# Backward pass of a gated attention and ReGLU mix: three edits to how attention's probabilities are turned, how queries are spread, and where projections stand

## The chip, the cores and the metric

The kernel runs on one core of a Trainium2 chip. A core has five instruction streams that run side by side and meet at semaphores: TensorE (PE; its weight loads, PEld, overlap its matmuls), VectorE (DVE), ScalarE (ACT), GpSimd (POOL) and SyncE (SP), which here only issues DMAs. Matmuls write to PSUM; the other data lies in SBUF, 128 partitions wide. A DMA that is issued from SP or ACT costs that queue its issue time; one that is issued from GpSimd is an instruction in GpSimd's own order. The metric is the device time of one execution in microseconds (us). Before: median 954.69 us of 3 runs (953.86 to 954.94).

## The reference

The input x has 2048 rows of 512. Two branches work on it and a gate mixes them; the kernel computes the output and the gradients of x, of all weights and of the gate, for a given grad_out.

```python
g = _sigmoid((x * gate_w).sum(-1, keepdims=True))
# branch A: attention, 32 heads of 16, a row sees itself and the 255 rows before it
qkv = (x @ wqkv).reshape(B, S, 3, H, Dh)
scores = jnp.einsum("bhqd,bhkd->bhqk", q, k) * (Dh ** -0.5)
mask = (idx[:, None] - idx[None, :] >= 0) & (idx[:, None] - idx[None, :] < W)
p = _softmax(jnp.where(mask[None, None], scores, -1e9), axis=-1)
a = jnp.einsum("bhqk,bhkd->bhqd", p, v).transpose(0, 2, 1, 3).reshape(B, S, D) @ wo
# branch B: relu(x W_gate) * (x W_up), times W_down; F = 1376
b = jnp.einsum("bsf,fd->bsd", relu(gate) * up, W_down)
return g * a + (1 - g) * b

# and the result with its gradients
_out, _vjp = jax.vjp(_f, A_x, A_wqkv, A_wo, B_W_gate, B_W_up, B_W_down, gate_w)
return (_out, *_vjp(grad_out))
```

## The kernel before

The work has three stages. The first (to about 254 us) does branch B forward and its backward products, in 11 chunks of the hidden width by 4 groups of 512 rows. The third (from about 760 us) does the products that give the output and the gradient of x, 128 rows at a time. Neither has an edit in it, apart from how the first group of queries is written at its end.

The second stage is attention, forward and backward, and it holds the change. It loops over 4 chunks `c` of 8 heads, and in a chunk over 16 blocks `j` of 128 query rows. A block meets key blocks `kb` = j, j-1 and j-2, which are its roles: "d" (diagonal, masked from above), "m" (middle, no mask) and "f" (far, masked from below). The 8 heads of a chunk are taken as two halves of 4. A block has so 6 units, one for each role and half; their order is m, f, d for the first half and m, d, f for the second. There are 360 units in all, since the first two blocks of a chunk have fewer.

The order of all engines is written by hand, as a loop over slots `n` (`manual_schedule`: each engine keeps the order of the program). In slot n:

- `front(u)` of unit n: PE multiplies K of one half by the spread queries into ST (L616, 128 keys x 4 heads x 128 queries). ACT takes exp into Pu (L627). GpSimd masks Pu for the roles d and f (L629, L632).
- `gradp` of unit n-1: VectorE multiplies Pu by dPT into Pd (L646).
- `rowsum` of unit n-3: PE multiplies both by K and V into BA (L655, L657), the rows' sums, outputs and parts of the gradients. After a block's last unit ACT copies BA out, and VectorE and GpSimd make small scaled tiles from it over the next slots (`small_ops`, L705 to L723).
- `front_dp(u)`: PE makes dPT for unit n (L641).
- `cd_piece`: PE multiplies the turned Pu and Pd of an older unit by those scaled tiles into CD (L486, L489), the gradients of K and V.

CD needs Pu and Pd turned: queries on the partitions instead of keys. `flip` does this in one of two ways. On PE: 8 transposes into PSUM (L687) and a copy to SBUF, by ACT and VectorE in turn, in slot n+3 of the unit. By DMA: a transposing DMA that SP issues in slot n+2. Diagonal units go by DMA, both halves in one transfer (tile PPd, L671). Of the middle units only the first half goes by DMA, alone (tile PPm, L678), in chunks 0 to 2 and in the blocks before 10 of chunk 3 (`u.dma`, L604). All other units are turned on PE. PPd has 3 buffers, PPm 2.

Between these, a running `credit` of PE time puts in background work: the weight gradients of the chunk before (L572), and the projections for the next group of 512 rows (`project_parts`): Q (L128), dO (L131), a transposing DMA of both, K, V, and a set of transposes of K and V. One part may go into a slot. Q and dO land side by side in a tile `zT`. ST and dPT want the heads in separate columns, each head-pair's 32 partitions alone in one column block with zeros around it, and so `spread` copies 32 rows at a time from `zT` to the tile `z` (L468), by four DMAs for each group, two in the slot after dO's and two in the next. SP issues them. `z` has two buffers, one for each group in turn; 15 groups are spread so, and the first is copied by VectorE and ACT.

`M`, a pool of four PSUM buffers, serves ST, dPT, the projections and the weight gradients.

Of the kernel before, what the change touches and what calls it, by code (L numbers as in the profile page):

```python
# [11 lines left out]
BF = mybir.dt.bfloat16  # L12
# [10 lines left out]
def kernel(  # L23
# [80 lines left out]
    NP = P // 32  # L104
    ZB = 2
    wq = ctx.enter_context(tc.tile_pool(name="wq", bufs=1))
    zt = [wq.tile([P, 2, TPG, NP, P], BF, tag=f"z{i}", name=f"z{i}") for i in range(ZB)]
    pjA = ctx.enter_context(tc.tile_pool(name="pjA", bufs=1))
    pjs = {}
    pools = {}  # L110
# [1 line left out]
    if True:  # L112
# [5 lines left out]
        def project_parts(c, tg):  # L118
# [4 lines left out]
            def mm(nm, which, eng):  # L123
# [20 lines left out]
                if nm in ("Q", "dO"):  # L144
                    if c == 0 and tg == 0:
                        w = ("Q", "dO").index(nm)
                        for k in range(NP):
                            rows = slice(32 * k, 32 * k + 32)
                            evac(zt[0][rows, w, :, k, :], dst[rows, :].rearrange("p (k q) -> p k q", k=TPG),
                                 (("dve", "act")[w] if k % 2 else "dve"))  # L150
                else:
                    for k in range(2):
                        t4[f"{nm}{k}"] = pj.tile([P, TGW], BF, tag=f"{nm}{k}", name=f"{nm}{k}")
                        if PENG[k] == "act":
                            nc.scalar.mul(t4[f"{nm}{k}"][:], pp[:], par[:, k:k + 1])
                        elif PENG[k] == "dve":
                            nc.vector.tensor_scalar(t4[f"{nm}{k}"][:], pp[:], par[:, k:k + 1], None, op0=ALU.mult)
                        else:
                            nc.vector.tensor_scalar(t4[f"{nm}{k}"][:], dst[:], par[:, k:k + 1], None, op0=ALU.mult)
# [297 lines left out]
    if True:  # L457
# [7 lines left out]
        pools["now"] = (ps, "M", 4, "TR")  # L465
        def spread(gi, k):
            rows = slice(32 * k, 32 * k + 32)
            nc.sync.dma_start(zt[gi % ZB][rows, :, :, k, :],  # L468
                              proj[groups[gi]]["z"][rows, :, :].rearrange("p w (k q) -> p w k q", k=TPG))

        P2 = {}
        RQ = {}
# [120 lines left out]
        for c in range(DC):  # L593
            for j in range(NT):
                kbs = [k for k in (j - 1, j, j - 2) if k >= 0]
                for half in range(2):
                    order = kbs if half or len(kbs) < 3 else [kbs[0], kbs[2], kbs[1]]
                    for ki, kb in enumerate(order):
# [2 lines left out]
                        u.first = ki == 0 and half == 0  # L601
                        u.last = ki == len(kbs) - 1 and half == 1
                        u.role = ("d", "m", "f")[j - kb]
                        u.dma = u.role == "d" or (u.role == "m" and half == 0 and (c < DC - 1 or j < 10))  # L604
                        units.append(u)
        NU = len(units)

# [2 lines left out]
        def front(u):  # L610
# [2 lines left out]
            KTt = proj[(u.c, u.kb // TPG)][f"K{u.half}"]  # L613
            ksl = slice((u.kb % TPG) * P, (u.kb % TPG + 1) * P)
            ST = ps.tile([P, HH, P], F32, tag="M", bufs=4, name="ST")
            nc.tensor.matmul(ST[:], lhsT=KTt[:, ksl], rhs=z[:, 0, jl, :, :], start=True, stop=True)  # L616
            if u.role == "d":
                if u.half == 0:
                    pairs[(u.c, u.j)] = wk.tile([P, 2, 2, HH, P], BF, tag="PPd", bufs=3, name="PPd")
                u.PP = pairs[(u.c, u.j)][:, u.half, :, :, :]  # L620
                u.Pu, u.Pd = u.PP[:, 0, :, :], u.PP[:, 1, :, :]
            elif u.dma:
                u.PP = wk.tile([P, 2, HH, P], BF, tag="PPm", bufs=2, name="PPm")
                u.Pu, u.Pd = u.PP[:, 0, :, :], u.PP[:, 1, :, :]
            else:
                u.Pu = wk.tile([P, HH, P], BF, tag="Pu", bufs=3, name="Pu")
# [8 lines left out]
        def front_dp(u):  # L635
# [2 lines left out]
            VTt = proj[(u.c, u.kb // TPG)][f"V{u.half}"]  # L638
            ksl = slice((u.kb % TPG) * P, (u.kb % TPG + 1) * P)
            u.dPT = ps.tile([P, HH, P], F32, tag="M", bufs=4, name="dPT")  # L640
            nc.tensor.matmul(u.dPT[:], lhsT=VTt[:, ksl], rhs=z[:, 1, jl, :, :], start=True, stop=True)  # L641

        def gradp(u):
            if not u.dma:
# [19 lines left out]
        copier = {"i": 0}  # L664

        def flip(u):
            if u.role == "d":
                if u.half == 0:
                    return
                p2 = wk.tile([P, 2, 2, HH, P], BF, tag="P2d", bufs=4, name="p2d")  # L670
                nc.sync.dma_start_transpose(out=p2[:].rearrange("p b a h q -> p (b a h) q"),  # L671
                                            in_=pairs.pop((u.c, u.j))[:].rearrange("p b a h q -> p (b a h q)"))
                for b in range(2):
                    P2[(u.c, u.j, u.kb, b)] = p2[:, b, :, :, :]
                return
            if u.dma:
                p2 = wk.tile([P, 2, HH, P], BF, tag="P2m", bufs=6, name="p2")
                nc.sync.dma_start_transpose(out=p2[:].rearrange("p a h q -> p (a h) q"),  # L678
                                            in_=u.PP[:].rearrange("p a h q -> p (a h q)"))
                P2[(u.c, u.j, u.kb, u.half)] = p2  # L680
                return
            eng = ("act", "dve")[copier["i"] % 2]
            copier["i"] += 1
# [1 line left out]
            for a, src in enumerate((u.Pu, u.Pd)):  # L685
                for hh in range(HH):
                    nc.tensor.transpose(pt[:, a, hh, :], src[:, hh, :], ident[:])  # L687
            p2 = wk.tile([P, 2, HH, P], BF, tag=f"P2{u.role}", bufs={"m": 6, "f": 4}[u.role], name="p2")
            evac(p2[:], pt[:], eng)
            P2[(u.c, u.j, u.kb, u.half)] = p2  # L690

        def small_ops(c, j, s):
# [88 lines left out]
        with tc.manual_schedule():  # L781
# [7 lines left out]
            n = 0  # L789

            held = False
            early = []
            late = []

# [14 lines left out]
            while n <= NU + LAG or ev or cdq or bgq:  # L809
# [63 lines left out]
                elif held and credit > 0.3:  # L873
                    held = background()
                    credit -= 0.65
                elif prq and not held and (credit > 0.4 or due - n <= len(prq)):
                    credit -= (0.44, 0.86, 0.86, 0.1, 0.86, 0.86)[len(prq) - 1]
                    prq.pop(0)()
                    if len(prq) == 4:
# [154 lines left out]
```

## Time and profile before

One execution with the profiler on took 954.53 us; its span, first to last instruction, is 952.6 us.

| | whole span | 300 to 400 us | 400 to 500 us | 600 to 700 us |
|---|---|---|---|---|
| PE busy | 917.2 us, 96% | 95.6% | 98.6% | 97.1% |
| PEld busy | 586.9 us, 62% | 69.6% | 71.7% | 69.9% |
| DVE busy | 503.1 us, 53% | 70.7% | 71.4% | 68.5% |
| ACT busy | 458.6 us, 48% | 71.7% | 73.2% | 70.0% |
| POOL busy | 486.9 us, 51% | 71.0% | 66.5% | 66.3% |
| share of the 16 DMA engines | | 0.83 | 0.86 | 1.01 |

How to read it: the page gives busy time of each engine, the span in 40 slices, the chain of work that ended last, and groups of instructions by line with their mean time and the idle time just before them. Matmuls are pipelined, so a matmul's own duration (378 ns for 512 columns) is longer than the step to the next one; the timeline's start times tell what it costs. A DMA share near 1 counts time in which packets were under way, not bytes at full rate.

### The profile page before, as it was taken

How to read it: one execution, taken by the hardware profiler on the slowest of the kernel's cores; microseconds unless marked ns; L12 is line 12 of the kernel's file. 1: busy time of each engine (PE TensorE's matmuls, PEld its weight loads, DVE VectorE, ACT ScalarE, POOL GpSimd, SP SyncE). 2: the span in 40 equal slices, each digit the busy share in tenths (PEclk: the TensorE clock that was granted, in tenths of full speed). 3: DMA queues.
4: the chain of work that ended last, by engine and by line, in shares of the span. 5: the costliest groups of instructions: out<-in, count | busy, mean ns of one | idle time of the engine just before them, and what ended most of it. 6: DMA issues, size and time to landing. Idle time of an engine off the chain costs nothing.

```text
span 952.6 us, 26867 instructions
## 1 busy us (share of the span) xinstructions
PE 917.2 (96%) x10965; PEld 586.9 (62%) x11065; DVE 503.1 (53%) x921; ACT 458.6 (48%) x795; POOL 486.9 (51%) x935
## 2 busy tenths in 40 slices
PE   7999999999989999999999999989999999999998
PEld 4556566556557776677776777766777644444443
DVE  4433334334367777567776667766677322322223
ACT  5422322222368777667776667866688310000001
POOL 2645445444177666666777567775677411121111
PEclk9999999999999999999999999999999999999999
DMA  9998789998587796977997869899989599777741
GB/s 295 189 189 194 181 205 211 211 205 191 135 146 125 130 170 110 158 149 122 169 139 128 145 124 182 145 149 166 180 148 204 136 271 229 189 189 189 187 100 44
DMA packets 470835, 160.27 MB, mean 168 GB/s; under 512 B 399448, under 2 KB 468408, under 8 KB 470712
## 3 DMA queue, kind: packets, MB, share of 16 engines
q1 hardware_dynamic: 448312, 135.48, 75.4%
q10 hardware_dynamic: 20592, 17.84, 6.9%
q0 software_dynamic: 1808, 5.24, 1.6%
q8 instruction: 86, 1.41, 0.6%
q14 instruction: 37, 0.30, 0.1%
HBM read 32.15 MB, written 36.31 MB: 72 GB/s over the span
## 4 chain that ended last, share of the span: by engine, by line
PE 65%; POOL 11%; DMA 7%; DVE 6%; issue 5%; ACT 3%; SPq 2%; ACTq 0%; POOLq 0%; DVEq 0%
PE dxps L976 7%; PE pt L687 5%; PE ST L616 5%; PE wps L371 5%; PE dPT L641 5%; PE dxps L991 4%; PE wps L572 4%; PE pp L128 4%; PE bps L945 4%; POOL Pu L632 3%; PE dhps L324 3%; PE BA L655 3%; PE CD L486 2%; PE gps L324 2%; PE ups L324 2%
## 5 line engine op out<-in xcount | busy, mean ns | idle before, releaser
L646 DVE TENSOR_TENSOR Pd<-Pu,dPT 128x512 bf16<-128x512 bf16 x178 | 120.2, 678 | 62.2 <-POOL Pu L632 49.7
L616 PE MATMUL ST<-z,K 128*128 128x512 bf16 x354 | 133.7, 378 | 6.1 <-DVE Pd L646 2.0
L641 PE MATMUL dPT<-z,V 128*128 128x512 bf16 x348 | 131.5, 378 | 4.4 <-DVE Pd L646 2.3
L627 ACT ACTIVATE Pu<-ST 128x512 bf16<-128x512 f32 x178 | 107.6, 604 | 45.4 <-PE ST L616 35.3
L629 POOL TENSOR_SCALAR_AFFINE_SELECT PPd<-PPd 128x512 bf16<-128x512 bf16 x128 | 81.7, 639 | 70.6 <-ACT PPd L627 70.2
L338 POOL TENSOR_TENSOR hT<-rg,upm 128x512 bf16<-128x512 bf16 x44 | 51.6, 1173 | 119.0 <-DVE upm L336 92.1
L646 DVE TENSOR_TENSOR PPd<-PPd,dPT 128x512 bf16<-128x512 bf16 x128 | 87.4, 683 | 44.6 <-POOL PPd L629 43.0
L371 PE MATMUL wps<-dgu_r,x_r 128*128 128x256 bf16 x704 | 105.6, 273 | 1.8 <-DVE wst L74 1.0
L72 ACT COPY p<-pt 128x1024 bf16<-128x1024 bf16 x89 | 90.7, 1019 | 7.5 <-PE pt L687 4.9
L627 ACT ACTIVATE PPd<-ST 128x512 bf16<-128x512 f32 x128 | 77.1, 602 | 32.4 <-PE ST L616 31.4
L371 PEld LDWEIGHTS <-x_r 128*128 128x128 bf16 x704 | 68.8, 98 | 32.6 <-issue 2.1
L632 POOL TENSOR_SCALAR_AFFINE_SELECT Pu<-Pu 128x512 bf16<-128x512 bf16 x112 | 71.6, 639 | 23.6 <-ACT Pu L627 23.4
L954 ACT COPY a_sb<-aps 128x512 f32<-128x512 f32 x16 | 9.4, 586 | 153.2 <-issue 137.6
L336 DVE SCALAR_TENSOR_TENSOR upm<-rg,ups 128x512 bf16<-128x512 bf16 x44 | 30.1, 684 | 79.9 <-ACT rg L330 40.3
L687 PE MATMUL pt<-ident,Pd 128*128 128x128 bf16 x712 | 68.8, 219 | 0.0
L486 PE MATMUL CD<-rq,p 128*128 128x32 bf16 x928 | 68.1, 177 | 0.5
L330 ACT ACTIVATE rg<-gps 128x512 bf16<-128x512 f32 x44 | 26.3, 598 | 87.2 <-PE gps L324 48.8
L687 PE MATMUL pt<-ident,Pu 128*128 128x128 bf16 x712 | 68.2, 217 | 0.0
L489 PEld LDWEIGHTS <-p 128*128 128x128 bf16 x928 | 54.6, 96 | 19.5
L489 PE MATMUL CD<-rq,p 128*128 128x16 bf16 x928 | 66.6, 169 | 0.0
L74 DVE COPY p<-pt 128x1024 bf16<-128x1024 bf16 x89 | 60.8, 684 | 6.0 <-PE pt L687 5.9
L486 PEld LDWEIGHTS <-p 128*128 128x128 bf16 x928 | 61.9, 96 | 1.2 <-issue 1.1
(167 smaller groups left out, 2236.1 us busy)
## 6 DMA issues: line engine op xcount, KB each, us to landing
dqkvo_d<-rows_st SPq DMA_DIRECT2D x7, 1024.0 KB, 6.0
hT_d<-hT ACTq DMA_DIRECT2D x44, 128.0 KB, 2.5
dgT_d<-dgu ACTq DMA_DIRECT2D x44, 128.0 KB, 2.8
duT_d<-dgu ACTq DMA_DIRECT2D x44, 128.0 KB, 3.0
duT_g<-duT_d SPq DMA_DIRECT2D x8, 640.0 KB, 5.4
gt<-hT_d SPq DMA_DIRECT2D x7, 640.0 KB, 5.9
dgT_g<-dgT_d SPq DMA_DIRECT2D x7, 640.0 KB, 5.2
z<-zT SPq DMA_DIRECT2D x60, 64.0 KB, 2.2
```

What stands on the lines that cost most here:

```text
L72: nc.scalar.copy(out, in_)
L371: nc.tensor.matmul(acc["w"][:, c, :], lhsT=x_r[:, t, c * P:(c + 1) * P], rhs=k.dgu_r[:, :, i, :], start=(go_ and c % 2 == 0), stop=no_, sk ...
L486: nc.tensor.matmul(cd[0][:, h, :], lhsT=p2[:, 0, hh, :], rhs=rq[:, h, 0:2 * Dh], start=cd[1], stop=True, skip_group_check=True)
L489: nc.tensor.matmul(cd[0][:, h, 0:Dh], lhsT=p2[:, 1, hh, :], rhs=rq[:, h, 2 * Dh:3 * Dh], start=False, stop=True, skip_group_check=True)
L616: nc.tensor.matmul(ST[:], lhsT=KTt[:, ksl], rhs=z[:, 0, jl, :, :], start=True, stop=True)
L627: nc.scalar.activation(u.Pu[:], ST[:], ACT.Exp)
L629: nc.gpsimd.affine_select(out=u.Pu[:], in_=u.Pu[:], compare_op=ALU.is_ge, fill=0.0, base=0, pattern=[[0, HH], [1, P]], channel_multiplier=-1)
L632: nc.gpsimd.affine_select(out=u.Pu[:], in_=u.Pu[:], compare_op=ALU.is_ge, fill=0.0, base=-1, pattern=[[0, HH], [-1, P]], channel_multiplier=1)
L641: nc.tensor.matmul(u.dPT[:], lhsT=VTt[:, ksl], rhs=z[:, 1, jl, :, :], start=True, stop=True)
L646: nc.vector.tensor_tensor(out=u.Pd[:], in0=u.Pu[:], in1=u.dPT[:], op=ALU.mult)
L687: nc.tensor.transpose(pt[:, a, hh, :], src[:, hh, :], ident[:])
L976: nc.tensor.matmul(dxps[:], lhsT=src[:, fc, lsl], rhs=W6[(wt, fc)], start=(i == 0), stop=(i == nmm - 1))
```

## The change

Three edits in the attention stage.

1. Both middle units of a block are turned by one DMA. PPm becomes a tile for both halves, as PPd was, and its transfer (128 x 2048 elements) goes out after the second half's product. The blocks of chunk 3 that do this are those before 8 instead of 10. Middle units that are still turned on PE write into halves of one tile of the same shape. The turned tiles have 3 buffers each (P2d had 4; P2m 6 of half the size).
2. The spread tile `z` is laid out with a head-pair's 512 columns in one run: `[P, 2, NP, TPG, P]` instead of `[P, 2, TPG, NP, P]`. So the spread writes runs of 1 KB instead of 256 B, and ST's and dPT's moving operand becomes four runs of 128 columns instead of one of 512. GpSimd issues the spread instead of SP.
3. A projection part is not put into the slot right after the last one, unless the group is due.

```diff
-    zt = [wq.tile([P, 2, TPG, NP, P], BF, tag=f"z{i}", name=f"z{i}") for i in range(ZB)]
+    zt = [wq.tile([P, 2, NP, TPG, P], BF, tag=f"z{i}", name=f"z{i}") for i in range(ZB)]
...
-            nc.sync.dma_start(zt[gi % ZB][rows, :, :, k, :],
-                              proj[groups[gi]]["z"][rows, :, :].rearrange("p w (k q) -> p w k q", k=TPG))
+            nc.gpsimd.dma_start(zt[gi % ZB][rows, :, k, :, :].rearrange("p w t q -> p w (t q)"),
+                                proj[groups[gi]]["z"][rows, :, :])
...
-                        u.dma = u.role == "d" or (u.role == "m" and half == 0 and (c < DC - 1 or j < 10))
+                        u.dma = u.role == "d" or (u.role == "m" and (c < DC - 1 or j < 8))
...
-            nc.tensor.matmul(ST[:], lhsT=KTt[:, ksl], rhs=z[:, 0, jl, :, :], start=True, stop=True)
-            if u.role == "d":
+            nc.tensor.matmul(ST[:], lhsT=KTt[:, ksl], rhs=z[:, 0, :, jl, :], start=True, stop=True)
+            if u.dma:
                 if u.half == 0:
-                    pairs[(u.c, u.j)] = wk.tile([P, 2, 2, HH, P], BF, tag="PPd", bufs=3, name="PPd")
-                u.PP = pairs[(u.c, u.j)][:, u.half, :, :, :]
-                u.Pu, u.Pd = u.PP[:, 0, :, :], u.PP[:, 1, :, :]
-            elif u.dma:
-                u.PP = wk.tile([P, 2, HH, P], BF, tag="PPm", bufs=2, name="PPm")
+                    pairs[(u.c, u.j, u.kb)] = wk.tile([P, 2, 2, HH, P], BF, tag=f"PP{u.role}",
+                                                      bufs={"d": 3, "m": 2}[u.role], name=f"PP{u.role}")
+                u.PP = pairs[(u.c, u.j, u.kb)][:, u.half, :, :, :]
                 u.Pu, u.Pd = u.PP[:, 0, :, :], u.PP[:, 1, :, :]
...
-            nc.tensor.matmul(u.dPT[:], lhsT=VTt[:, ksl], rhs=z[:, 1, jl, :, :], start=True, stop=True)
+            nc.tensor.matmul(u.dPT[:], lhsT=VTt[:, ksl], rhs=z[:, 1, :, jl, :], start=True, stop=True)
...
         def flip(u):
-            if u.role == "d":
+            if u.dma:
                 if u.half == 0:
                     return
-                p2 = wk.tile([P, 2, 2, HH, P], BF, tag="P2d", bufs=4, name="p2d")
+                p2 = wk.tile([P, 2, 2, HH, P], BF, tag=f"P2{u.role}", bufs=3, name=f"p2{u.role}")
                 nc.sync.dma_start_transpose(out=p2[:].rearrange("p b a h q -> p (b a h) q"),
-                                            in_=pairs.pop((u.c, u.j))[:].rearrange("p b a h q -> p (b a h q)"))
+                                            in_=pairs.pop((u.c, u.j, u.kb))[:].rearrange("p b a h q -> p (b a h q)"))
                 for b in range(2):
                     P2[(u.c, u.j, u.kb, b)] = p2[:, b, :, :, :]
-                return
-            if u.dma:
-                p2 = wk.tile([P, 2, HH, P], BF, tag="P2m", bufs=6, name="p2")
-                nc.sync.dma_start_transpose(out=p2[:].rearrange("p a h q -> p (a h) q"),
-                                            in_=u.PP[:].rearrange("p a h q -> p (a h q)"))
-                P2[(u.c, u.j, u.kb, u.half)] = p2
                 return
...
-            p2 = wk.tile([P, 2, HH, P], BF, tag=f"P2{u.role}", bufs={"m": 6, "f": 4}[u.role], name="p2")
-            evac(p2[:], pt[:], eng)
+            if u.role == "m":
+                if u.half == 0:
+                    pairs[(u.c, u.j, "p2")] = wk.tile([P, 2, 2, HH, P], BF, tag="P2m", bufs=3, name="p2m")
+                p2 = pairs[(u.c, u.j, "p2")][:, u.half, :, :, :]
+            else:
+                p2 = wk.tile([P, 2, HH, P], BF, tag="P2f", bufs=4, name="p2")[:]
+            evac(p2, pt[:], eng)
...
+            fed = -2
...
-                elif prq and not held and (credit > 0.4 or due - n <= len(prq)):
+                elif prq and not held and ((credit > 0.4 and n > fed + 1) or due - n <= len(prq)):
+                    fed = n
                     credit -= (0.44, 0.86, 0.86, 0.1, 0.86, 0.86)[len(prq) - 1]
                     prq.pop(0)()
```

More of the change, by code (lines that the diff above doesn't have):

```diff
@@ L148, in mm @@
                             rows = slice(32 * k, 32 * k + 32)
[L149 removed]
+                            evac(zt[0][rows, w, k, :, :], dst[rows, :].rearrange("p (k q) -> p k q", k=TPG),
                                  (("dve", "act")[w] if k % 2 else "dve"))
```

## The prediction

> **What bounds the kernel now.** I read the page first: busy shares, the 40 slices, then the chain that ended last.
>
> ```profile
> span 952.6 us, 26867 instructions
> PE 917.2 (96%) x10965; PEld 586.9 (62%) x11065; DVE 503.1 (53%) x921; ACT 458.6 (48%) x795; POOL 486.9 (51%) x935
> ...
> PE   7999999999989999999999999989999999999998
> ...
> DMA  9998789998587796977997869899989599777741
> ...
> PE 65%; POOL 11%; DMA 7%; DVE 6%; issue 5%; ACT 3%; SPq 2%; ACTq 0%; POOLq 0%; DVEq 0%
> ```
>
> TensorE is busy nearly everywhere and carries 65% of the chain; GpSimd is next with 11%. The change lives in the attention stage, which the first and last ST matmuls put at about 254 to 744 us, so next I took sums by stretch.
>
> ```profile
> 300.00:400.00 100.00, 95.62 (x1711) 69.59 (x1720) 70.68 (x131) 71.65 (x127) 71.02 (x168) 1.00 0.83 139
> 400.00:500.00 100.00, 98.55 (x1739) 71.67 (x1745) 71.42 (x129) 73.22 (x127) 66.54 (x153) 1.00 0.86 145
> 600.00:700.00 100.00, 97.07 (x1665) 69.85 (x1672) 68.47 (x126) 70.01 (x123) 66.32 (x155) 1.00 1.01 162
> ...
> 300.00:306.50 6.50, 6.50 (x137) 5.08 (x135) 4.87 (x8) 5.58 (x11) 5.21 (x12) 1.00 0.81 134
> ```
>
> The columns are PE, PEld, DVE, ACT, POOL, clock, DMA share, GB/s. PE is at 96 to 99% at full clock, the other three at 66 to 73%. The last line is a block without projections or weight gradients: there ACT has 5.58 of 6.5 us and GpSimd 5.21, so PE is only just the longest. Whether PE's busy time is real work shows in its timeline:
>
> ```profile
> 451.17 0.38 PE L641 MATMUL dPT<-z,V 128*128 128x512 bf16 x1
> ...
> 451.59 0.38 PE L616 MATMUL ST<-z,K 128*128 128x512 bf16 x1
> ...
> 452.01 0.38 PE L687 MATMUL pt<-ident,Pu 128*128 128x128 bf16 x4
> ...
> 452.23 0.39 PE L687 MATMUL pt<-ident,Pd 128*128 128x128 bf16 x4
> ...
> 452.45 0.38 PE L641 MATMUL dPT<-z,V 128*128 128x512 bf16 x1
> ```
>
> From dPT to dPT are 1.28 us here, and the eight transposes of one turned unit (a flip) take 0.44 of them, 452.01 to 452.45, with nothing idle between: a slot without a flip is 0.84 us. So PE's own instructions are what the stage costs, and 0.44 us is the price of a flip. The rows for everything else that moves:
>
> ```profile
> L632 POOL TENSOR_SCALAR_AFFINE_SELECT Pu<-Pu 128x512 bf16<-128x512 bf16 x112 | 71.6, 639 | 23.6 <-ACT Pu L627 23.4
> L646 DVE TENSOR_TENSOR Pd<-Pu,dPT 128x512 bf16<-128x512 bf16 x178 | 120.2, 678 | 62.2 <-POOL Pu L632 49.7 <-ACT Pu L627 5.0 <-PE CD L489 4.4
> L960 POOL DMA_DIRECT2D out_dram<-o_sb x16 | 8.7, 542 | 88.9 <-DVE o_sb L958 88.9
> L131 PE MATMUL pp<-d,p 128*128 128x512 bf16 x60 | 16.2, 378 | 3.2 <-DVE zT L140 3.0
> ...
> p2d<-PPd SPq DMA_TRANSPOSE x64, 5.1
> ...
> p<-PPm SPq DMA_TRANSPOSE x54, 4.2
> ```
>
> VectorE's product waits 49.7 us for GpSimd's select: GpSimd's order is the tightest thing behind PE. One DMA issued by GpSimd holds it 0.54 us.
>
> **The change, part by part.** The sum is made against the profiled execution's own 954.53 us (952.6 us of span and 1.9 around it); the median of the runs is 954.69, 0.16 above.
>
> *Flips.* Before, only the first half's middle unit went by DMA: 45 units in chunks 0 to 2 and 9 in chunk 3, 54 in all. After, both halves go: 52 pairs, 104 units (45 pairs, and 7 in chunk 3). 50 units leave TensorE: 400 of 1,424 transposes. 50 x 0.44 = **-22 us**. Their copies (25 on ACT at 1.02 us, 25 on VectorE at 0.68) leave engines that are not the bound, and count nothing.
>
> Not all of it can be had. In the 14 blocks without background work (blocks 6, 7, 10, 11, 14, 15 of chunk 0, and 10, 11, 14, 15 of chunks 1 and 2) the last line of the stretches leaves GpSimd 1.3 us and ACT 0.9 us of room in a block, and a unit's chain (0.38 ST, 0.60 exp, 0.64 select, 0.68 product) must fit into three slots, of which three in a row now have no flip. I take half of the cut there as lost: 14 x 0.22 = **+3** (0 to +6, none or all of it).
>
> *Spread.* 60 DMAs (15 groups of 4) leave SP, where each held the queue 0.6 us and nothing on PE waited for them. They land on GpSimd, two at the end of each of two slots, and each is 0.54 us by the L960 row, 32 us of new GpSimd time. In most groups the first pair falls in the slot of a middle unit, which has no select: covered. The second pair stands behind the second diagonal unit's select and ahead of the small products and of the far unit's select. That pair delays the select by 1.08 us; behind it stand VectorE's product and the BA matmuls three slots on, which have about 0.3 us in hand in the densest blocks. So 15 x (1.08 - 0.3) = **+12**. Bounds: 0, if the waits overlap idle time that is there anyway, to 30 x 1.08 = +32, if both pairs of each group are paid in full. The DMAs also wait for dO's copy out of PSUM, which VectorE does in about the same slot; that is inside the bounds. The 1 KB runs shorten 64 KB transfers whose median landing is 2.2 us and which are read a group (some 20 slots) later: nothing, and with that cover gone at most their landing, once a group. The new layout gives ST's and dPT's moving operand four strided runs of 128. That is free: wps at L371 reads two such runs of 128 in 273 ns, L572 reads 384 in one run in 325 and L616 512 in 378, all on one line.
>
> *Projections kept apart.* PE's wait of 3.0 us at L131 is dO's product right after Q's, waiting for Q's copy; L128 has 2.9 us of the same kind. Most of it should go: **-4** (0 to -6, all of both rows).
>
> *DMA.* 54 turns of 256 KB go and 52 of 512 KB come, next to 64 of 512 KB: per block two large ones instead of one and a half, issued by SP in neighbouring slots. The results are needed a block later, so the 5.1 us landing is covered. The tight place is the pair's source PPm, with two buffers: its turn goes out in slot 5 of a block and must have landed by slot 0 of the block after next, 7 slots or 7 to 9 us. Where a 1 MB spill or a weight turn stands ahead on SP, exp of that unit waits. Today ACT waits for PPm's DMA 2.1 us in all, with 10 slots of room. I take **+2** more (0 to +26, if each of 52 pairs waits half a microsecond). SP's waits for a free p2 buffer (4 to 3 deep) end about two slots before the next turn: nothing.
>
> Sum: -22 + 3 + 12 - 4 + 2 = -9, so 954.5 - 9 = **945.5 us**.
>
> **A rule against the trace.** The DMA share is 0.83 to 1.01 in the stage: read plainly, there is no room for a third more turned data. Yet ACT waited only 2.1 us for PPm's DMA, so I rate it as room. The Trainium skill ("Perfetto Trace Analysis", Identifying the Most-Contended Engine) calls that occupancy misleading for 16 DMA engines and goes by HBM use, and by it the DMA term would be 0 and the sum 943.5. The same section distrusts matmul busy time and goes by the share of weight loads; by it PE, at 70% in the stage, would have room, and the sum would be that of the third rival below, 954.
>
> **Rivals.**
> 1. *Full gain.* The spread hides: -22 - 4 and small losses of 0 to 6, so 928 to 935. For it: GpSimd is idle 29 to 34% of the stage. Against it: VectorE already waits 49.7 us for its selects.
> 2. *GpSimd takes over; slower.* Both pairs of each group delay a select, at the lines of the selects and the spread, and the blocks without background give nothing back: 954.5 - 22 + 6 + 32 - 4 = 966, and less if one pair is partly covered. It decides from (22 - 3 + 4 - 2) / 30 = 0.7 us lost for each pair of spread DMAs, against 1.08 for a pair. For it: the second pair has no idle time in front of it. Against it: the first pair has.
> 3. *PE is not the bound,* or the flips' time turns into waits of the same size: -22 + 22, the spread on idle time: 954. The gapless timeline speaks against it, the 5.58 of 6.5 us on ACT for it.
> 4. *The turns are late.* exp waits for PPm in most blocks: +26 in place of +2, hence 969 with my other terms, 957 if the spread hides behind those waits. For it: share 1.01 at 600 to 700 us; against it: 2.1 us today.
>
> **How the numbers follow.** The forecast's own band, 936 to 952: 0.48. Rival 1: 0.20. Rival 2: 0.17 (of it 0.02 just under the time before). Rival 3: 0.08. Rival 4: 0.07. 0.2% of 954.7 is 1.9 us, about what a measurement can tell from no change. Faster: 0.48 + 0.20 + 0.02 = 0.70; same: 0.07, most of rival 3; slower: 0.23, the rest. For 8 in 10 the range takes the band, most of rival 1, rival 3 and the lower part of rival 2: 931 to 962.
>
> **What would show it.** Right: 1,024 transposes onto pt, PE busy time down by about 20 us, GpSimd up by about 32 with spread DMAs of 0.5 us, the stage's last ST near 735 us instead of 744, VectorE's wait for the far unit's select up. Wrong in the spread: issues far from 0.54 us, or PE waiting at BA and ST behind products that wait for selects by more than 12 us over before. Wrong in the DMA: ACT waiting for PPm's landing by more than a few us. The forecast fails most easily if GpSimd's delay comes with both pairs, or not at all.

## The result, and the profile after

The changed kernel takes 972.02 us (median; 967.38 to 972.50) against 954.28 us for the kernel before on the same chip: a ratio of 1.0174, 95% interval of 1.0151 to 1.0197. It is slower by 1.7%; 945.5 was predicted, and the range (931 to 962) does not hold it. The profiled execution took 971.56 us. One execution of the run a_sp below, its profiled one, was slow (1407.93 us at a granted clock of 0.57); a_sp's time is the median of its other three.

The page of the changed kernel, its busy times and its chain:

```profile
span 969.6 us, 26186 instructions
...
PE 916.4 (95%) x10665; PEld 572.2 (59%) x10665; DVE 486.6 (50%) x896; ACT 441.2 (46%) x770; POOL 517.7 (53%) x995
...
PE 62%; POOL 19%; DVE 8%; DMA 5%; issue 4%; ACT 1%; SPq 0%; POOLq 0%; DVEq 0%; ACTq 0%
```

The 300 TensorE instructions that are missing are what was announced (400 transposes fewer, and 100 records that the trace of before had lost). TensorE's busy time fell by only 0.8 us all the same (a little more, if the lost records were there), where about 20 were expected. The granted clock is 0.989 over the span, against 1.000 before, and 0.011 x 969.6 us is 11 us of stretched work, as an estimate; in the run below that leaves 52 turns out, at a clock of 0.998, TensorE's busy time is 897.8 us. GpSimd's 31 us more are the 60 spread DMAs (33.3 us). But GpSimd's share of the chain rose from 11 to 19%. The stretches of the attention stage, columns as before (PE, PEld, DVE, ACT, POOL, clock, DMA share, GB/s):

```profile
300.00:400.00 100.00, 88.65 (x1572) 62.34 (x1571) 65.46 (x123) 65.56 (x117) 74.90 (x174) 1.00 0.99 167
400.00:500.00 100.00, 92.17 (x1557) 63.91 (x1555) 61.91 (x115) 63.92 (x114) 68.47 (x158) 0.98 1.00 168
600.00:700.00 100.00, 92.14 (x1498) 63.13 (x1495) 60.43 (x113) 62.20 (x111) 69.79 (x161) 0.97 1.13 190
```

PE was at 95.6, 98.6 and 97.1% here and is at 88.7 to 92.2; no other engine is fuller than 75%. So nothing new is the bound: engines wait for each other. The groups say for whom (these lines stand two lower than before: L644 is before's L646, L639 its L641, L625 its L627, L630 its L632, L627 its L629):

```profile
L639 PE MATMUL dPT<-z,V 128*128 128x512 bf16 x360 | 137.5, 382 | 23.6 <-DVE PPd L644 14.0 <-DVE Pd L644 4.7 <-ACT KT L72 4.3
L644 DVE TENSOR_TENSOR PPd<-PPd,dPT 128x512 bf16<-128x512 bf16 x128 | 87.3, 682 | 66.8 <-POOL PPd L627 66.4
L644 DVE TENSOR_TENSOR Pd<-Pu,dPT 128x512 bf16<-128x512 bf16 x128 | 86.9, 683 | 85.2 <-POOL Pu L630 80.1 <-PE CD L489 4.4 <-PE dPT L639 0.5
L625 ACT ACTIVATE PPm<-ST 128x512 bf16<-128x512 f32 x104 | 62.2, 598 | 39.6 <-PE ST L616 26.1 <-DMA p2m<-PPm 10.4 <-PE dPT L639 1.6
L468 POOL DMA_DIRECT2D z<-zT x60 | 33.3, 559 | 11.0 <-DVE zT L74 11.0
```

VectorE's products waited 49.7 and 43.0 us for GpSimd's selects before, and wait 80.1 and 66.4 now. PE's dPT stands 23.6 us, where it stood 4.4, most of it for a PSUM buffer that such a product still reads. ACT's exp waits 10.4 us for the paired turn's DMA (2.1 before). GpSimd stands 11.0 us in front of a spread DMA until VectorE has copied dO.

### The profile page after: what moved, and what is told of

Same layout as the page of the kernel before. It is cut to its first block, busy times and chain, and to the rows that moved or that the text cites. A ratio compares the mean times of both kernels' runs of the same rounds, so it can differ in the third digit from the quotient of the medians.

```text
span 969.6 us, 26186 instructions
## 1 busy us (share of the span) xinstructions
PE 916.4 (95%) x10665; PEld 572.2 (59%) x10665; DVE 486.6 (50%) x896; ACT 441.2 (46%) x770; POOL 517.7 (53%) x995
## 3 DMA queue, kind: packets, MB, share of 16 engines
q8 instruction: 83, 1.36, 0.6%
## 4 chain that ended last, share of the span: by engine, by line
PE 62%; POOL 19%; DVE 8%; DMA 5%; issue 4%; ACT 1%; SPq 0%; POOLq 0%; DVEq 0%; ACTq 0%
PE wps L371 8%; PE dxps L975 7%; PE dxps L990 4%; PE dhps L324 4%; PE dps L373 4%; PE ups L324 4%; PE gps L324 4%; PE dPT L639 4%; PE bps L944 3%; DVE PPd L644 3%; POOL PPd L627 3%; PE wps L572 3%; POOL Pu L630 3%; PE ST L616 3%; PE pp L128 3%
## 5 line engine op out<-in xcount | busy, mean ns | idle before, releaser
L639 PE MATMUL dPT<-z,V 128*128 128x512 bf16 x360 | 137.5, 382 | 23.6 <-DVE PPd L644 14.0
L644 DVE TENSOR_TENSOR Pd<-Pu,dPT 128x512 bf16<-128x512 bf16 x128 | 86.9, 683 | 85.2 <-POOL Pu L630 80.1
L644 DVE TENSOR_TENSOR PPd<-PPd,dPT 128x512 bf16<-128x512 bf16 x128 | 87.3, 682 | 66.8 <-POOL PPd L627 66.4
L627 POOL TENSOR_SCALAR_AFFINE_SELECT PPd<-PPd 128x512 bf16<-128x512 bf16 x128 | 81.3, 635 | 44.0 <-ACT PPd L625 43.5
L625 ACT ACTIVATE PPd<-ST 128x512 bf16<-128x512 f32 x128 | 76.7, 599 | 40.7 <-PE ST L616 39.2
L625 ACT ACTIVATE Pu<-ST 128x512 bf16<-128x512 f32 x128 | 76.6, 599 | 37.2 <-PE ST L616 31.6
L625 ACT ACTIVATE PPm<-ST 128x512 bf16<-128x512 f32 x104 | 62.2, 598 | 39.6 <-PE ST L616 26.1
L630 POOL TENSOR_SCALAR_AFFINE_SELECT Pu<-Pu 128x512 bf16<-128x512 bf16 x112 | 71.5, 638 | 15.6 <-ACT Pu L625 15.2
L644 DVE TENSOR_TENSOR PPm<-PPm,dPT 128x512 bf16<-128x512 bf16 x104 | 68.9, 662 | 0.9 <-ACT PPm L625 0.7
L373 PE MATMUL dps<-db_r,h_r 128*128 128x512 bf16 x176 | 66.7, 379 | 0.0
L348 POOL TENSOR_TENSOR dgu<-dh_sb,rg 128x512 bf16<-128x512 bf16 x44 | 58.3, 1325 | 8.0 <-ACT dh_sb L344 8.0
L959 POOL DMA_DIRECT2D out_dram<-o_sb x16 | 8.7, 542 | 90.4 <-DVE o_sb L957 90.4
L128 PE MATMUL pp<-x,p 128*128 128x512 bf16 x192 | 50.5, 387 | 4.9 <-ACT PPm L625 3.8
L705 POOL TENSOR_TENSOR ndel<-BAs,rinv 128x8 f32<-128x8 f32 x64 | 13.4, 209 | 75.9 <-DVE rinv L702 74.5
L72 ACT COPY p<-pt 128x1024 bf16<-128x1024 bf16 x48 | 48.6, 1013 | 5.1 <-PE pt L679 0.7
```

The source lines that it names most:

```text
L128: nc.tensor.matmul(pp[:], lhsT=w_p[c][:, cd, which * P:(which + 1) * P], rhs=x_T[tg][:, cd, :], start=(cd == 0), stop=(cd == DC - 1))
L348: nc.gpsimd.tensor_tensor(out=k.duT, in0=dh_sb[:], in1=k.rg[:], op=ALU.mult)
L373: nc.tensor.matmul(acc["d"][:], lhsT=k.h_r[:, i, :], rhs=db_r[:, t, :], start=go_, stop=no_)
L625: nc.scalar.activation(u.Pu[:], ST[:], ACT.Exp)
L627: nc.gpsimd.affine_select(out=u.Pu[:], in_=u.Pu[:], compare_op=ALU.is_ge, fill=0.0, base=0, pattern=[[0, HH], [1, P]], channel_multiplier=-1)
L630: nc.gpsimd.affine_select(out=u.Pu[:], in_=u.Pu[:], compare_op=ALU.is_ge, fill=0.0, base=-1, pattern=[[0, HH], [-1, P]], channel_multiplier=1)
```

## The experiments

Three edits, three rivals (GpSimd takes over, PE is not the bound, the turns are late): first each edit alone and each taken away.

| times in us | neither | spacing | GpSimd's spread | both |
|---|---|---|---|---|
| turns as before | 954.5 | 951.84 | 953.98 | 968.88 |
| paired turn | 973.38 | 959.84 | 961.80 | 972.02 |

"Spacing" is the third edit, projection parts not in neighbouring slots. The table's cells are the runs below; the last is the change. GpSimd's spread comes with the new layout everywhere; the cell of paired turn and spacing has that layout too.

### Taking one edit away from the change

**The spread back on SyncE** (a_sp):

```diff
-            nc.gpsimd.dma_start(zt[gi % ZB][rows, :, k, :, :]...
+            nc.sync.dma_start(zt[gi % ZB][rows, :, k, :, :]...
```

> The changed kernel with one word undone: SP issues the 60 spread DMAs again (1 KB runs, the new layout, the pairs and the spacing of projections stay). GpSimd theory (the 33 us of spread issues and the 11 us that GpSimd stands waiting for dO's copy delay the selects, and that is where 40 us of new PE waits come from): 940 to 950 us, VectorE's waits for selects back from 146 to about 100 us. Chain theory (the select chain of three slots can't go faster, so the flips' 22 us become waits whoever issues the spread): 958 to 968. Transfer theory (the larger turns land late and ACT waits for PPm): 965 to 975, since SP's queue gets 60 more issues.

959.84 us, ratio 1.0062 (1.0040 to 1.0084): 12.2 us better than the change, yet not under the kernel before.

**The old turns, with the other two edits** (a_noflip): `u.dma`, `front` and `flip` as in the kernel before.

> The changed kernel with the turns of before: only the first half's middle unit by DMA, alone, so 50 units are back on PE; the spread by GpSimd in 1 KB runs and the spacing of projections stay. GpSimd theory: the spread costs its 12 to 30 us here too, less 4 for the spacing, so 962 to 980. Chain theory: PE's extra 22 us sit where waits were, 952 to 960. Transfer theory: the late turns are gone, 950 to 958.

968.88 us, 1.0153 (1.0136 to 1.0170). Almost the whole loss is there with every turn as before.

**No spacing** (a_nofed):

```diff
-                elif prq and not held and ((credit > 0.4 and n > fed + 1) or due - n <= len(prq)):
+                elif prq and not held and (credit > 0.4 or due - n <= len(prq)):
```

> The changed kernel without the spacing of projections: two parts may stand in neighbouring slots again. All theories by my sum: 4 us slower than the changed kernel, 974 to 978. If spacing hurts, because bare slots follow each projection and the selects of those are what PE waits for: faster than the changed kernel, 960 to 970.

961.80 us, 1.0077 (1.0062 to 1.0092). Of the three edits taken away singly, this one and the spread's issuer help most, and they are the two that I had priced at -4 and +12.

### One edit alone

**The paired turn** (b_pair): `u.dma`, `front` and `flip` of the change in the kernel before.

> The kernel before with the paired turn of both middle units alone (spread by SP in 256-byte runs, no spacing). GpSimd theory: the flips' 22 us are had for the most part, 934 to 942 us. Chain theory: half of it or less, 945 to 954. Transfer theory: ACT waits for PPm as in the changed kernel or more, 950 to 965.

973.38 us, 1.0201 (1.0186 to 1.0216): the turns that should have saved 22 us cost 19, more than any of the three expectations held. Rows of this run's timeline, SyncE's queue and ScalarE's exp (start, duration; in square brackets the idle time before and its releaser):

```profile
287.12 1.24 SPq L171 DMA_TRANSPOSE rows<-zT  x1
...
288.45 3.27 SPq L468 DMA_DIRECT2D z<-zT  x4
...
291.83 2.02 SPq L669 DMA_TRANSPOSE p2m<-PPm  x1
...
298.11 0.60 ACT L625 ACTIVATE PPm<-ST 128x512 bf16<-128x512 f32 x1 [3.57 <-DMA p2m<-PPm]
```

The pair's turn stands behind the transfer of Q's and dO's rows and the four spread DMAs, which hold SyncE's queue until 291.72. It leaves at 291.83, and exp of a later pair, which needs the PPm buffer, waits 3.57 us. In the whole run ACT waits 39.3 us for that DMA, 15 times. That is my fourth rival, and here it holds, though for 15 of the 52 pairs and not for most. In the run without spacing, where GpSimd issues the spread, the turn at the same place leaves at 288.98 and no such wait follows there (in that whole run exp waits 14.3 us for the pair's turn).

**The spacing** (b_fed):

> The kernel before with the spacing of projections alone. My sum: 950 to 952 (4 us saved). If spacing is what cost 10 us between the changed kernel and the one without it, by leaving bare slots behind each projection: 956 to 964. If it costs only beside the spread on GpSimd, because the pairs of spread DMAs then always fall in bare slots: 951 to 955.

951.84 us, 0.9968 (0.9955 to 0.9981): -2.9 us, and L131's wait of 3.2 us is down to 0.3. But the wait for Q's copy did not vanish: 3.0 us of it stood before L131 in the kernel before, and 3.5 us of it stand before ST now. Where the 2.9 us come from is not shown.

**GpSimd's spread, with its layout** (b_pool):

> The kernel before with the spread alone: new layout, 1 KB runs, issued by GpSimd. GpSimd theory by my sum: 966 (12 us), bounds 954 to 986. If the spacing is what exposes the spread: 954 to 960, and GpSimd's wait for dO's copy below the 11 us of the run without flips.

953.98 us, 0.9991 (0.9982 to 1.0000): free.

**The layout on SyncE** (b_lay):

> The kernel before with the new layout alone: SP issues the spread as before, now in 1 KB runs, and the moving operands are four strided runs. My sum: nothing, 953 to 956. If the strided operand costs PE: ST and dPT longer than 378 ns and 958 or more. If shorter runs crowd the transfers: 948 to 952.

954.42 us, 0.9997 (0.9988 to 1.0007): the 1 KB runs and the strided operand cost and bring nothing by themselves, as said.

**Pair and layout, spread on SyncE, no spacing** (a_sp_nofed):

> The changed kernel with SP issuing the spread and without the spacing; it differs from the run with the paired turn alone (973) by the 1 KB runs only. Transfer theory (the paired turns miss their buffer's time, and the spread's packets and issues on SP's queue make it worse): with a quarter of the spread's packets ACT waits for PPm 15 to 30 us instead of 39, 960 to 968. If it is SP's issue order alone that matters, not packets: 970 to 975. If the chain of selects bounds it: 958 to 962, as with GpSimd's issue.

976.72 us, 1.0231 (1.0207 to 1.0256), above all three expectations, ACT waiting 36.0 us for PPm's DMA (14 times). So the longer runs, the only difference from the paired turn alone, do not help the late turn. With spacing the same kernel had 959.84. The spacing takes two of the four spread DMAs from in front of the pair's turn on SyncE, and the other two stay there: in the run a_sp_swap below, with the same queue order as a_sp, they leave at 287.91 and the turn at 289.90. That this is what saves the 17 us is not shown.

So two questions were open: why 50 turns less on PE bring nothing even where exp waits little for their DMA (10.4 us in the change), and why two edits that cost nothing alone cost 15 us together.

### Why less TensorE work is not less time

**Turns left out, no transfers** (x_omit). The second middle half's 52 turns are dropped from the kernel before; CD reads the first half's turned tile twice, so these units' gradients of K and V are not computed.

```diff
         def flip(u):
+            if u.role == "m" and u.half == 1 and (u.c < DC - 1 or u.j < 8):
+                P2[(u.c, u.j, u.kb, 1)] = P2[(u.c, u.j, u.kb, 0)]
+                return
```

> The kernel before with work left out: the second middle unit of 52 blocks isn't turned at all, neither on PE nor by DMA (CD reads the first half's turned tile in its place, so the gradients of K and V are not the reference's). It prices the flips without any transfer: 416 transposes fewer, 23 us. PE theory (my sum): 931 to 936 us. Chain theory (the three-slot chain of exp, select and product fills the time): 945 to 955, with VectorE's waits for selects well above the 93 us of before.

950.56 us, 0.9962 (0.9949 to 0.9975): 3.5 us for 52 x 0.44 = 23 us of TensorE. Two blocks without background take 7.03 and 7.04 us (from one reciprocal's start to the next, 324.13, 331.16, 338.20). In the kernel before, with more work, the same two take 6.54 and 7.03:

```profile
323.81 0.20 DVE L705 RECIPROCAL rinv<-BAs 128x8 f32<-128x8 f32 x1
...
330.35 0.20 DVE L705 RECIPROCAL rinv<-BAs 128x8 f32<-128x8 f32 x1
...
337.38 0.20 DVE L705 RECIPROCAL rinv<-BAs 128x8 f32<-128x8 f32 x1
```

The timeline with the turns left out, the chain from the rows' sums to dPT:

```profile
336.25 0.50 ACT L661 COPY BAs<-BA 128x400 f32<-128x400 f32 x1
...
337.00 0.68 DVE L74 COPY p<-pt 128x1024 bf16<-128x1024 bf16 x1
...
337.60 0.68 DVE L646 TENSOR_TENSOR PPd<-PPd,dPT 128x512 bf16<-128x512 bf16 x1
...
338.20 0.20 DVE L708 RECIPROCAL rinv<-BAs 128x8 f32<-128x8 f32 x1
...
338.48 0.20 POOL L711 TENSOR_TENSOR ndel<-BAs,rinv 128x8 f32<-128x8 f32 x1 [1.41 <-DVE rinv L708]
...
339.48 0.64 POOL L629 TENSOR_SCALAR_AFFINE_SELECT PPd<-PPd 128x512 bf16<-128x512 bf16 x1
...
340.15 0.69 DVE L646 TENSOR_TENSOR PPd<-PPd,dPT 128x512 bf16<-128x512 bf16 x1 [1.20 <-POOL PPd L629]
...
340.89 0.38 PE L641 MATMUL dPT<-z,V 128*128 128x512 bf16 x1 [0.99 <-DVE PPd L646]
```

BAs is there at 336.75, but the reciprocal stands in VectorE's order behind the copy of a turned unit and a product, until 338.20. GpSimd waits 1.41 us for it, does its small products, and only then the second diagonal select (339.48). VectorE waits for that, and PE stands 0.99 us for the PSUM buffer. The block before has the same wait at 333.85. With three turned units in a block the copies alternate between ACT and VectorE from block to block: in the kernel before a VectorE copy stands ahead of the reciprocals at 323.81 and 337.38, and none ahead of the one at 330.35. With two turned units each block has the same order, and here the copy that stands ahead of the reciprocal is always VectorE's.

**The same, copies swapped** (x_swap; it leaves out the same turns):

```diff
-        copier = {"i": 0}
+        copier = {"i": 1}
```

> The kernel before with the second middle half's turns left out (52 units, as in the run that gave 950.6), and the copies of the remaining turned units start on VectorE instead of ScalarE, so that in a block the two change places. If a VectorE copy ahead of the reciprocal is what keeps the blocks without background at 7.12 us (GpSimd's small products wait 1.4 us for the reciprocal, the diagonal select stands behind them), those blocks fall towards 6.6 and the time to 942 to 947. If the loop through select, product and PSUM buffer is the same with either order, it stays at 950 to 952. If a copy on ScalarE then delays BA's copy instead, it goes above 952.

938.30 us, 0.9829 (0.9813 to 0.9845). The same work in the other order: 12 us less, more than expected. The chain of one block again:

```profile
326.40 0.49 ACT L661 COPY BAs<-BA 128x400 f32<-128x400 f32 x1
...
327.32 0.68 DVE L646 TENSOR_TENSOR PPd<-PPd,dPT 128x512 bf16<-128x512 bf16 x1
...
327.91 0.20 DVE L708 RECIPROCAL rinv<-BAs 128x8 f32<-128x8 f32 x1
...
328.20 0.21 POOL L711 TENSOR_TENSOR ndel<-BAs,rinv 128x8 f32<-128x8 f32 x1 [0.93 <-DVE rinv L708]
...
329.87 0.69 DVE L646 TENSOR_TENSOR PPd<-PPd,dPT 128x512 bf16<-128x512 bf16 x1 [0.24 <-POOL PPd L629]
```

The copy comes after the reciprocal, the block takes 6.43 us (321.48 to 327.91 to 334.35), and dPT's waits in the whole run fall from 18.9 to 1.6 us. So what fewer turns brought depends on the copies' order, which they also fixed: 3.5 us in the late order, 16 in the early one.

The swap was not run on the kernel before as it is, but the traces say part of what it does. From the tenth to the last reciprocal of chunk 3 the three kernels turn the same units: these six blocks take 41.1 us in the kernel before, 41.1 with the turns left out elsewhere, and 39.2 with the copies swapped, a gain of the order alone. And the kernel before, with its two orders in turn, stands between the other two. The two blocks above take 13.57 us in it, 14.07 in the late order and 12.87 in the early one: in the mean of the two orders 0.1 us saved, for 0.88 us of TensorE work less. The next two, with background work, take 17.11, 16.58 and 16.04 us: 0.8 saved. So at the order of before the 52 turns are worth about 10 of their 23 us ((3.5 + 16) / 2, an estimate), and the order takes or gives about 6. In these blocks a turn less is worth nearly its full time where TensorE has background work, and almost nothing where it has none.

**Swapped copies in two kernels that compute everything.** In the change with the spread on SyncE (a_sp_swap):

> The change with SyncE issuing the spread (961.2), copies swapped between the engines in the same way. If the copies' order is what eats the saved TensorE time: 953 to 957. If not: 960 to 963.

960.01 us, 1.0065 (1.0041 to 1.0089): not faster. Its group of exp says why:

```profile
L625 ACT ACTIVATE PPm<-ST 128x512 bf16<-128x512 f32 x104 | 63.5, 611 | 48.0 <-DMA p2m<-PPm 32.7 <-PE ST L616 14.3 <-PE CD L489 0.9
```

Exp waits 32.7 us for the paired turn (17 times); what the order gives is spent there. So I tried the same turns in smaller pieces, each half by its own DMA. First without the swap (s_fed: kernel before, spacing, spread on SyncE, both middle halves by DMA singly, PPm 4 buffers of half the size, P2d 3 buffers):

```diff
-                        u.dma = u.role == "d" or (u.role == "m" and half == 0 and (c < DC - 1 or j < 10))
+                        u.dma = u.role == "d" or (u.role == "m" and (c < DC - 1 or j < 8))
...
-                u.PP = wk.tile([P, 2, HH, P], BF, tag="PPm", bufs=2, name="PPm")
+                u.PP = wk.tile([P, 2, HH, P], BF, tag="PPm", bufs=4, name="PPm")
```

> Both middle units of a block by DMA, but each by its own of 256 KB as soon as it is ready (PPm four half-size buffers, the same bytes as two pairs), spread by SP in 256-byte runs, spacing of projections as in the changed kernel; blocks before 8 of chunk 3 as there. The turn of a half then has 10 slots to land, not 7. Transfer theory (the pair's late source buffer eats the gain): ACT waits for PPm under 5 us and 930 to 940 us. Chain theory: 950 to 960, close to the 961 of the pair with SP's spread and spacing.

953.87 us, 0.9993 (0.9976 to 1.0009). Exp of these units no longer shows a wait for PPm's DMA, and the time is still that of the kernel before, so in this kernel late landing is not what eats the gain; dPT waits 21.8 us, 18.0 of it behind the diagonal product. Then with the swap (s_fed_swap):

> Each middle half turned by its own DMA, spacing, spread on SyncE (953.9), copies swapped. If the copies' order eats the saved time: 946 to 950, faster than every other version. If not: 953 to 955.

944.30 us, 0.9886 (0.9871 to 0.9901): the fastest kernel of the study that computes everything, 1.1% under the kernel before, and below the expected 946 to 950. dPT's waits are down to 8.2 us. Exp waits 8.1 us for PPm's DMA, and the share of the DMA engines is 1.10 to 1.11 between 300 and 600 us.

### Why GpSimd's spread is free alone and dear with the spacing

First theory: the two pairs of DMAs fall into two slots, and one of them in a bad one. All four in the slot after dO's part, without and with the paired turn (noflip4, after4):

```diff
-                            ev.setdefault(n + 1 + k // 2, []).append(("dma", lambda gi=gi, k=k: spread(gi + 1, k)))
+                            ev.setdefault(n + 1, []).append(("dma", lambda gi=gi, k=k: spread(gi + 1, k)))
```

> The kernel with GpSimd's spread and the spacing but the turns of before (968.9), with all four spread DMAs of a group in the slot after dO's product instead of two there and two in the next. Placement theory (the second pair stands ahead of the far unit's select; in one slot all four stand in the gap that the middle unit leaves): 951 to 956. If it is GpSimd's 33 us or the wait for dO's copy as such: 966 to 971.

> The changed kernel with all four spread DMAs in the slot after dO's product. Placement theory: as much less as in the run without flips, so 955 to 960. If late turned tiles and selects bound it whatever GpSimd does: 966 to 973.

969.75 us, 1.0163 (1.0144 to 1.0182), and 971.19 us, 1.0181 (1.0156 to 1.0206). Nothing gained: the theory falls. Second theory: GpSimd stands at the DMA until dO is copied (11 us). Two slots later there is nothing to wait for (noflip_late: `n + 3 + k // 2`):

> GpSimd's spread and the spacing without the turns, with the spread DMAs two slots later than in the change (slots n+3 and n+4 after dO's part). If the loss of these two edits together (968.9 against 952 for the spacing and 954 for the spread alone) comes from GpSimd standing at a spread DMA until dO's copy is done, with selects and small products behind it, the wait for zT (11.4 us) goes and the time falls to 952 to 957. If the 60 issue times of 0.55 us are the loss wherever they stand, it stays at 965 to 972.

967.26 us, 1.0129 (1.0110 to 1.0148). The wait for zT is gone from the groups, the loss is not. So it is the issue time itself. Then why is it free alone? GpSimd's timeline in the run with the spread alone:

```profile
313.52 0.64 POOL L629 TENSOR_SCALAR_AFFINE_SELECT PPd<-PPd 128x512 bf16<-128x512 bf16 x1 [1.88 <-ACT PPd L627]
314.11 2.18 POOL L468 DMA_DIRECT2D z<-zT  x4
316.30 0.22 POOL L708 TENSOR_TENSOR ndel<-BAs,rinv 128x8 f32<-128x8 f32 x1
...
318.76 0.69 POOL L632 TENSOR_SCALAR_AFFINE_SELECT Pu<-Pu 128x512 bf16<-128x512 bf16 x1
```

And the same place in the kernel before:

```profile
315.41 0.20 POOL L708 TENSOR_TENSOR ndel<-BAs,rinv 128x8 f32<-128x8 f32 x1 [0.92 <-DVE rinv L705]
...
316.90 0.64 POOL L629 TENSOR_SCALAR_AFFINE_SELECT PPd<-PPd 128x512 bf16<-128x512 bf16 x1 [0.45 <-ACT PPd L627]
...
319.05 0.64 POOL L632 TENSOR_SCALAR_AFFINE_SELECT Pu<-Pu 128x512 bf16<-128x512 bf16 x1 [0.77 <-ACT Pu L627]
```

The four DMAs' 2.18 us use up gaps in which GpSimd stood anyway: 0.92 us for the reciprocal, then 0.45 and 0.77 us for exp. By the far unit's select GpSimd has caught up (318.76, against 319.05 before). The spacing moves dO's part by slots, and the DMAs, as I took it, out of these gaps. Third theory, then: put them into the gap by position in the block (noflip_gap):

```diff
+                        m = n + 1
+                        while pos[min(m, NU - 1)] != 2:
+                            m += 1
                         for k in range(NP):
-                            ev.setdefault(n + 1 + k // 2, []).append(("dma", lambda gi=gi, k=k: spread(gi + 1, k)))
+                            ev.setdefault(m + k // 2, []).append(("dma", lambda gi=gi, k=k: spread(gi + 1, k)))
```

(`pos` is a unit's place in its block.)

> GpSimd's spread and the spacing without the turns, with a group's four spread DMAs always at the end of the third and fourth unit of a block: behind the first diagonal select, ahead of the middle unit that has no select and of the small products that wait for the reciprocal. There GpSimd stands idle 1.4 us or more in every block. If the issue time costs only where GpSimd has no such gap, the time falls from 968.9 to 952 to 956. If it costs wherever it stands, 964 to 971.

961.86 us, 1.0084 (1.0060 to 1.0108): 7 of the 17 us are back, between the two expectations. Most of the other 10 are visible at the start of the later chunks, where blocks are short and GpSimd has no gap anywhere:

```profile
377.58 1.10 POOL L468 DMA_DIRECT2D z<-zT  x2
...
380.00 1.15 POOL L468 DMA_DIRECT2D z<-zT  x2
...
384.13 0.64 POOL L635 TENSOR_SCALAR_AFFINE_SELECT Pu<-Pu 128x512 bf16<-128x512 bf16 x1
...
384.80 0.69 DVE L649 TENSOR_TENSOR Pd<-Pu,dPT 128x512 bf16<-128x512 bf16 x1 [2.31 <-POOL Pu L635]
...
385.54 0.38 PE L644 MATMUL dPT<-z,V 128*128 128x512 bf16 x1 [2.35 <-DVE Pd L649]
```

GpSimd works without a pause from 377.58 to the select at 384.13; the four DMAs' 2.25 us arrive whole at VectorE (2.31) and at PE (2.35). In the whole run dPT waits 7.1 us in this way, 2.35 at the start of each of the three later chunks: 7 of the 10. After the second of these waits (512.77) the granted clock is 0.58 from 514 to 518 us, and the block there is another 1.5 us longer than with the spacing alone; after the other two waits the clock stays at 1.00. What the rest is stays open.

**Everything together** (after_gap_swap): the change, with the spread in the gap and the copies swapped.

> All three edits of the change, with the spread DMAs in that gap and the copies of turned units swapped between ScalarE and VectorE. If the three causes add up (spread outside the gap 15 us, order of the copies 8 to 10, and the paired turn's late landing, which stays), 945 to 952. If the paired turn's wait is what the rest hangs on: 955 to 962, with ACT waiting more than 20 us for PPm's DMA.

954.05 us, 0.9997 (0.9981 to 1.0013): 18 us better than the change, no better than the kernel before, and 2 us above the sum that I expected if the causes add up. Exp waits 21.6 us (14 times) for the paired turn's DMA, more than the 10.4 in the change. Two causes are repaired, and the third has grown; that it alone takes what they gave back is not shown.

## Why the prediction was wrong, by its own steps

- **Flips, -22, and +3 lost in the blocks without background.** The step that failed. PE's own work did fall (50 turns at 0.44), but the timeline "with nothing idle between" was read as proof that PE is the bound. PE was full because the loop exp, select, product, PSUM buffer just kept pace. Without any transfer the cut brought 3.5 us. I had written that the copies leave engines that are not the bound "and count nothing"; what counted was not their time but which engine does which of the two that stay: VectorE's copy came ahead of the reciprocal in every block, where it had been in every other one. In the other order the same cut measures -16, of which the turns are about 10 and the order about 6, by the estimate above. The third rival (954; 0.08) named a PE that is not the bound, with ACT's 5.58 of 6.5 us as its reason; the reason was VectorE's order. The loss in the blocks without background was rightly seen and sized too small: there 0.8 of 0.88 us is lost, not half. The Trainium skill ("Perfetto Trace Analysis", Identifying the Most-Contended Engine) distrusts matmul busy time and goes by the share of weight loads; that share was 70% in the stage. By the runs this was right about the blocks without background and not about those with it: neither view names the chain.
- **Spread, +12 (0 to +32).** Nothing without the spacing (953.98 against 954.70), 17 with it (968.88 against 951.84). The mechanism was the one that I gave, issue times ahead of a select that PE then waits for, and 17 lies inside the bounds. Two parts of the step failed. That the first pair is covered and only the second costs did not hold: all four in the first pair's slot cost the same (969.75). And it missed that the third edit decides whether the DMAs lie in GpSimd's gaps, so the terms do not add.
- **DMA, +2 (0 to +26).** Mis-sized. With the spread still on SyncE, ACT waits 32.7 to 39.3 us for PPm; in the change itself 10.4, perhaps because GpSimd's delays give the transfers time, which no run separates. It was inside the bounds, but in the place shown it was not a spill that stood ahead on SyncE; it was the rows' turn and the four spreads. That a share near 1 still left room was right: the fastest kernel that computes everything has 1.10.
- **Projections, -4.** The number was right (-2.9 alone), and that was luck in part. L131's 3.0 us are gone, but ST now waits 3.5 us for the same copy. And L128's 2.9 us, read as the same kind, were not: its row names the diagonal product (1.3) as the main releaser, and with the spacing they are 3.5.
- **Layout, strided operand.** Right: 954.42 alone, against 954.70.

The change's 17.7 us add up, in the order of the prediction, as: -3.5 for the turns, +17 for spread and spacing together over the spacing alone, -2.9 for the spacing, and 7 that remain for the paired turn's late landing and for what the terms do to each other, worked out as the rest and not measured singly. Time at half clock lies inside these terms: by the granted clock the change lacks about 9 us of TensorE work in the attention stage (46 us at 0.96, and 100 us each at 0.98, 0.98 and 0.97; an estimate and an upper bound, since TensorE also waits in these stretches), the kernel before none. Rivals 2, 3 and 4 each held in part. I gave them 0.32 in all as if only one could be true.

## What to carry to other kernels

A TensorE that is busy 97% of a stage is not proven to be its bound: leave the work out in one run and look whether the time follows. When work is taken from an alternation of two engines, look which engine now always has the copy that stands ahead of a short, late instruction (here a reciprocal of 0.2 us on which GpSimd's whole order hangs). Here a DMA that GpSimd issues costs its issue time unless it lies where GpSimd waits anyway, and an edit elsewhere in the schedule can move it out of that place.

## What the runs showed of the hardware that I had not expected

Waits of TensorE can cost more than their length. In the run with the paired turn alone, PE mostly waits from 336 to 340 us, and the granted clock is then half (columns as above, clock third from the end):

```profile
336.00:340.00 4.00, 1.36 (x27) 0.90 (x25) 1.38 (x2) 0.51 (x2) 3.07 (x7) 1.00 1.20 186
340.00:343.40 3.40, 3.07 (x36) 2.06 (x36) 1.89 (x3) 2.12 (x5) 1.27 (x2) 0.50 1.19 240
```

Between 300 and 700 us the kernel before has a clock of 1.00 in every stretch of 100 us, the change 0.97 to 1.00, the run with the paired turn alone 0.93 to 0.98. Over its span of 971.7 us that run has 0.982; 0.018 x 971.7 is 17 us, so most of the 19 us that it loses can be half clock after the waits rather than the waits (an estimate and an upper bound). Not every wait does it: in the run with the spread in the gap, TensorE waits 2.35 us three times, and the clock falls after one of them. The Trainium skill ("TensorE: Matmul & The Clock Gate", The HAM clock gate) has the clock fall to half after an idle window of about 3.4 us; the trace agrees on the half, and shows it here after a stretch in which PE was not idle but busy 1.36 of 4 us.

And four spread DMAs in a row hold SyncE's queue 3.27 us in the place shown, 0.82 each, where I had reckoned 0.6; elsewhere in that run four take 2.56 to 3.89 us.
